# Weight loads on ScalarE's queue, with a planner that knows two queues, in a fused attention and feed-forward kernel

## The chip, the cores and the metric

The kernel runs on one core of one Trainium2 chip. The metric is the device time of one execution in microseconds (us): the median of three runs. The engines are named as the profile names them: PE is TensorE's matmul, PEld its weight load, DVE is VectorE, ACT is ScalarE, POOL is GpSimd, SP is SyncE, whose queue issues DMA transfers. All arithmetic runs in float32; a "split" operand is held as a rounded high part and a low part, so that two or three fast matmuls give a float32 product.

## The reference

The inputs are q, k, v of 4 batches x 8 heads x 576 positions x 64, a memory `M_prev` (64 x 64) and `z_prev` (64) per head, `beta` per head, and the weights `w_in` (512 x 2048) and `w_out` (2048 x 512), which come as float64.

```python
scores = where(causal, -1e9, (q @ k.T) / 8); a = softmax(scores); local = a @ v
q_p = where(q > 0, q, exp(q) - 1) + 1
mem_out = (q_p @ M_prev) / (q_p . z_prev + 1e-6)
attn = g * mem_out + (1 - g) * local            # g = sigmoid(beta), per head
x = attn as 2304 tokens x 512
h = x @ w_in;  g = where(h > 0, h, exp(min(h, 0)) - 1)
out = g @ w_out
```

## The kernel before

The 2304 tokens are cut into nine groups of 256: unit 0 holds the first 64 positions of the four batches, the units 1 to 4 the next 256 positions of one batch each, the units 5 to 8 the last 256. A unit's attention runs over four pairs of heads, and its result is the 512-wide x of the group, split into `xh` and `xl`. The feed-forward of a group runs over 16 chunks of 128 hidden columns: `add_ff` multiplies x by a chunk of `w_in` into the PSUM tile h (L901), applies the elu (ACT L916; DVE L919, L922), splits the result into `gh` (L931) and `gl` (L934) and accumulates its product with the chunk of `w_out` (L965). The groups named by `SPLIT` run their first chunks early and the others later, so that feed-forward work starts while only a few chunks of the weights are ready; the half sums go out to a buffer `part` and come back.

The weights arrive as float64 and are turned into split float32 on the core, piece by piece: 32 pieces (16 chunks of each matrix), 128 x 1024 int32 words each, 512 KB. `add_weights` issues the load into the staging tile `st` (L379; two buffers), then scales the exponent word (rebias, L385, L387 or L389 on ACT, DVE or POOL), isolates the sign (L396 or L398), merges the low word (L403, L406, both on DVE), rounds the high part (L409) and subtracts for the low part (L412). The join L406 is the last reader of the staging buffer, which then takes the load after the next.

In attention, `add_phi` makes q_p (ACT L464, DVE L467 to L496, DVE or POOL L485); unit 0 goes through `add_first` (score matmuls L588, masked reductions L592, exponentials L607, transposes L636, products L651), the others through `add_pair` (scores L787 or L819, reductions L801, exponentials L832, scaling L848, transposes L878, copies L884, products L739). `add_mem` puts the memory's factor beside the probabilities (L545, on DVE or POOL).

Nothing of this is issued in the order of the code. Each operation is handed to a planner (`Plan`), with a priority, the tiles it reads and writes, and one or more engines that could run it, each with an assumed duration. `Plan.order` then keeps one clock per engine and always takes the operation that can begin first, the lower priority number first among equals; of several engines it takes the one that ends first after a bonus in `BIAS`. The order in which it takes them is the order of the instructions on each engine's queue, which is fixed. Where PE would stand idle before the first feed-forward accumulation, the planner puts in warm-up matmuls that compute nothing (L1033). The numbers at the top of the file (`A_OFF`, `V_OFF`, `E_OFF`, `UDUE`, `UBEG`, `W_ADD`, `P_ADD`, `W_LATE`, `SPLIT`) shift priorities: of the units, of the loads of v, of the elu, of the single weight pieces. All DMA transfers stand on SP's queue. An issue waits on its queue until its buffer is free, and what is queued behind it waits too.

## Time and profile before

| what | us |
|---|---|
| time, median of 3 runs (lowest, highest) | 599.02 (598.54, 599.17) |
| profiled execution, its own time | 599.39 |
| its span (first to last instruction) | 597.6 |
| busy in the span: PE | 586.7 (98%) |
| busy: DVE | 442.0 (74%) |
| busy: ACT | 381.1 (64%) |
| busy: POOL | 73.0 (12%) |
| issues of weight loads, first to last start | 3.1 to 158.9 |

Busy times are the union of an engine's instructions; DMA issues, waits and branches are not counted as busy. Matmuls are pipelined, so PE counts as busy while its pipeline is not full. The granted clock of PE is full in all stretches up to the last 20 us. A row of the chain of waits gives the share of a stretch in which the chain that ended last ran on that line; the idle time in brackets of a timeline row is the idle time of that engine before the instruction, with what ended it.

### The profile page before, as it was taken

Reading aid. Unit: us, or ns where it says so; the run is one execution under the profiler, and the core shown is the slowest. Engines: PE = TensorE matmul, PEld = TensorE weight load, DVE = VectorE, ACT = ScalarE, POOL = GpSimd, SP = SyncE. Lnnn points to the kernel's source line nnn. Section 1 sums busy time; section 2 is a strip of 40 time slices with the busy share of each in tenths; the row PEclk is TensorE's granted clock in tenths of the full one; section 3 lists DMA queues with packets and bytes.
Section 4 is the critical chain, followed back from the end, with each engine's and each line's share of the span. In section 5 each row is a group of like instructions: output and inputs, shape, how many; then the busy total and the mean of one; then the engine's idle time right before and its main releaser. Section 6 shows DMA issues by size and latency. Waiting matters only on the chain.

```text
span 597.6 us, 11969 instructions
## 1 busy us (share of the span) xinstructions
PE 586.7 (98%) x4150; PEld 507.0 (85%) x4150; DVE 442.0 (74%) x1394; ACT 381.1 (64%) x1021; POOL 73.0 (12%) x108
## 2 busy tenths in 40 slices
PE   8999999999999999999999999999999999999997
PEld 6766868898898898999888999898889888899996
DVE  6999999999987884477774478687968786444443
ACT  5699889676677872377682377686767776533222
POOL 3333123120011120000120000101111010000000
PEclk9999999999999999999999999999999999999999
DMA  8755756445463332012422022424232323000000
GB/s 264 234 189 183 220 158 209 160 163 185 144 184 113 96 127 72 1 59 90 137 74 59 1 94 74 117 72 154 73 118 74 103 92 103 1 2 28 10 1 36
DMA packets 32813, 63.85 MB, mean 107 GB/s; under 512 B 3568, under 2 KB 17392, under 8 KB 32752
## 3 DMA queue, kind: packets, MB, share of 16 engines
q1 hardware_dynamic: 32752, 63.08, 33.5%
q8 instruction: 33, 0.54, 0.4%
q14 instruction: 28, 0.23, 0.1%
HBM read 56.77 MB, written 6.29 MB: 106 GB/s over the span
## 4 chain that ended last, share of the span: by engine, by line
PE 83%; DVE 12%; ACT 2%; issue 1%; DMA 1%; POOL 0%; DVEq 0%; ACTq 0%; POOLq 0%; SPq 0%
PE acc L965 31%; PE h L901 31%; PE t L739 7%; PE t L878 7%; PE s L787 6%; DVE p L801 2%; DVE st L403 1%; PE acc L1033 1%; DVE wf L406 1%; ACT p L848 1%; DMA p<-in_kqf 1%; DVE gl L934 1%; DVE e L919 1%; DVE p L545 1%; DVE qp L470 1%
## 5 line engine op out<-in xcount | busy, mean ns | idle before, releaser
L901 PE MATMUL h<-xh,w1h 128*128 128x256 f32 x576 | 149.4, 284 | 0.5 <-DVE e L922 0.5
L901 PE MATMUL h<-xl,w1h 128*128 128x256 f32 x576 | 148.1, 281 | 0.0
L901 PEld LDWEIGHTS h<-xh,w1h 128*128 128x128 f32 x576 | 108.4, 188 | 11.9 <-DVE e L922 1.0
L901 PEld LDWEIGHTS h<-xl,w1h 128*128 128x128 f32 x576 | 108.9, 189 | 9.6
L916 ACT ACTIVATE e<-h 128x256 f32<-128x256 f32 x144 | 55.1, 383 | 64.7 <-PE h L901 64.0
L931 ACT CAST gh<-e 128x256 fp32r<-128x256 f32 x143 | 57.8, 404 | 59.2 <-DVE e L922 56.4
L965 PE MATMUL acc<-w2h,gl 128*128 128x512 f32 x288 | 93.5, 403 | 0.0
L965 PE MATMUL acc<-w2h,gh 128*128 128x512 f32 x288 | 92.4, 402 | 0.4 <-ACT gh L931 0.4
L965 PE MATMUL acc<-w2l,gh 128*128 128x512 f32 x288 | 92.8, 402 | 0.0
L901 PEld LDWEIGHTS h<-xh,w1l 128*128 128x128 f32 x576 | 85.0, 189 | 9.2 <-issue 0.5
L901 PE MATMUL h<-xh,w1l 128*128 128x256 f32 x576 | 92.7, 283 | 0.0
L832 ACT ACTIVATE p<-p,mn 128x192 f32<-128x192 f32 (+3 forms) x128 | 78.6, 616 | 18.1 <-DVE mn L801 17.9
L919 DVE TENSOR_SCALAR e<-e 128x256 f32<-128x256 f32 x144 | 43.7, 303 | 51.8 <-ACT e L916 50.4
L934 DVE TENSOR_TENSOR gl<-e,gh 128x256 fp32r<-128x256 f32 x131 | 57.3, 438 | 31.7 <-ACT gh L931 30.9
L884 ACT COPY pth<-t 128x384 f32<-128x384 f32 (+2 forms) x155 | 67.2, 455 | 11.5 <-PE t L878 10.4
L878 PE MATMUL t<-ident,p 128*128 128x128 f32 x448 | 69.3, 274 | 1.2 <-POOL p L852 0.6
L801 DVE CUSTOM_DVE_ANT_0 p<-s,mask 128x192 f32<-128x192 f32 (+3 forms) x128 | 57.9, 476 | 14.8 <-PE s L787 9.7
L878 PEld LDWEIGHTS t<-ident,p 128*128 128x128 f32 x448 | 53.5, 140 | 12.4 <-ACT p L848 2.2
L922 DVE SCALAR_TENSOR_TENSOR e<-h,e 128x256 f32<-128x256 f32 x144 | 60.6, 421 | 2.2
L739 PE MATMUL t<-pth,v 128*64 128x256 f32 (+1 forms) x512 | 54.5, 357 | 1.7 <-ACT pth L884 1.7
L739 PEld LDWEIGHTS t<-pth,v 128*64 128x64 f32 x512 | 34.9, 137 | 20.8 <-ACT pth L884 3.4
L848 ACT ACTIVATE p<-p,rs 128x320 f32<-128x320 f32 (+3 forms) x88 | 47.1, 584 | 6.6 <-DVE rs L556 5.2
(97 smaller groups left out, 818.6 us busy)
## 6 DMA issues: line engine op xcount, KB each, us to landing
kq<-in_kq SPq DMA_DIRECT2D x32, 416.0 KB, 3.1
st<-in_w_in SPq DMA_DIRECT2D x16, 512.0 KB, 3.4
st<-in_w_out SPq DMA_DIRECT2D x16, 512.0 KB, 3.6
qz<-in_qzx SPq DMA_DIRECT2D x32, 224.0 KB, 2.9
v<-in_vx SPq DMA_DIRECT2D x32, 160.0 KB, 2.4
out<-st SPq DMA_DIRECT2D x16, 256.0 KB, 2.1
kq<-in_kqp SPq DMA_DIRECT2D x12, 288.0 KB, 3.3
v<-in_vx SPq DMA_DIRECT2D x16, 192.0 KB, 3.4
```

Source lines behind the costliest of these rows:

```text
L739: nc.tensor.matmul(ps.t[64 * j:64 * j + 64, G * n + lo:G * n + G], vj.t[:, v0 + c], tj.t[:, o:o + G - lo], start=(i == 0), stop=(i == len( ...
L801: nc.vector.tensor_tensor_reduce(out=pts[i].t[:, po + 64 + a:po + 64 + e], in0=ps.t[:, o:o + e - a], in1=m, op0=ALU.add, op1=ALU.min, scal ...
L832: nc.scalar.activation(out=x, in_=x, func=AF.Exp, bias=mn.t[:, 0:1], scale=-1.0, accum_out=rs.t[:, col:col + 1])
L848: eng.activation(out=x, in_=x, func=AF.Copy, scale=c)
L878: nc.tensor.matmul(ps.t[:, 128 * (c - a):128 * (c - a) + 128], pt.t[:, po + 128 * c:po + 128 * c + 128], ident, start=True, stop=True, is_ ...
L884: return lambda: eng(dst(), ps.t[:, 0:n].rearrange("p (c q) -> p c q", q=128))
L901: nc.tensor.matmul(ps.t[:, 0:G], w[:, c, k], x.t[:, k], start=(k == 0 and w is w1h and x is xh), stop=(k == 3 and lo))
L916: nc.scalar.activation(out=at(ee), in_=ps.t[:, 0:G], func=AF.Exp)
L922: nc.vector.scalar_tensor_tensor(at(gg), ps.t[:, 0:G], 0.0, e.t, ALU.max, ALU.add)
L931: return lambda: eng(gh.t, at(gg))
L934: return lambda: eng.tensor_tensor(gl.t, at(gg), gh.t.bitcast(F32), op=ALU.subtract)
L965: nc.tensor.matmul(acc[t].t, a.t[:, 128 * t:128 * t + 128], w[:, c], start=(c == c0 and i == 0), stop=(c == c1 - 1 and i == 2))
```

## The change

The load of a weight piece is issued by `nc.scalar` in place of `nc.sync`, so it stands on ACT's queue. The planner gets a second queue, "Q2", which takes 1587 ns per piece as SP did, and for the issue 330 ns of ACT's time; the transfer follows the issue without delay, and its data counts as landed 2600 ns after its end. In the planner both queues have the full rate. Thirteen of the constants at the top are set anew; `PS_FROM`, `RELU_FF` and `PHI_MIN` are among them, which select nothing at the old or the new value. Line numbers below the table of latencies grow by 3 or 4 (L379 becomes L382, L464 becomes L468).

```diff
--- before.py
+++ after.py
@@ -28,31 +28,31 @@
 SIGN = -0x80000000
 REBIAS = 2.0 ** -112
 MASKED = -8e9
-A_OFF = 11
-PS_FROM = 276
+A_OFF = 12
+PS_FROM = 252
 TURN_S = 400.0
 TURN_V = 370.0
 NATIVE = (1, 1, 1, 1, 0, 0, 0, 0, 0)
 PV_TWO = [0, 0, 0, 1, 1, 1, 1, 1, 1]
 RUN_SPLIT = (((0, 0, 192),), ((1, 0, 320),)), (((0, 0, 448),), ((1, 0, 288),), ((1, 288, 576),))
 CLOCK_OFF = 450.0
-V_OFF = 80
+V_OFF = 65
 SN = 2
 TN = 2
-SPLIT = (4, 7, 11)
-UDUE = (-29, 4, 17, 55, 62, 81, 65, 101, 114)
-UBEG = (-44, -1, 11, 22, -4, 67, 91, 58, 99)
+SPLIT = (4, 8, 11)
+UDUE = (-21, 4, 17, 55, 62, 80, 69, 104, 112)
+UBEG = (-50, 0, 12, 22, -12, 67, 89, 61, 99)
 RB = {'mn': 10, 'rs': 4, 'p': 2, 'pth': 4, 'v': 4, 'ks': 1, 'qh': 1, 'ql': 1, 'kq': 1, 'ev': 3}
-BIAS = {'POOL': -400, 'DVE': -150, 'DV2': -250, 'ACT': -750}
-E_OFF = 162
+BIAS = {'POOL': -400, 'DVE': 50, 'DV2': -250, 'ACT': -750}
+E_OFF = 190
 FIRST_ACT = 4
 W_FIRST = -970
-RELU_FF = -20
+RELU_FF = -22
 RELU_PHI = 0
-PHI_MIN = -1
-W_LATE = (1, 0, -4, -14)
-W_ADD = (0, 6, -1, 0, -1, -2, -8, 3, 1, -3, -3, -1, 5, 11, -8, 0, 4, -5, 1, 8, 16, -16, -5, 2, -10, 1, 2, 7, -10, -18, 1, 1)
-P_ADD = (-19, -2, 17, 2, -1, 0, -1, 1, 0, -1, 0, 0, 0, -1, -1, -2, -10, 18, -15, -1, 0, 0, 1, -17, 0, -10, 7, -7, 10, -2, 8, 9, 5, 10, 0, -1)
+PHI_MIN = 0
+W_LATE = (0, 0, -7, -15)
+W_ADD = (-11, 14, -1, 2, 15, -2, -16, 3, 9, -3, -11, -2, 5, 5, -5, -1, 4, -6, 1, 15, 16, -8, 6, 2, -1, 2, 2, 18, -8, -20, -5, -1)
+P_ADD = (-11, 8, 24, 7, -1, 0, -1, 9, 0, -2, 3, 0, 0, 7, -1, -2, -11, 20, -15, -3, -3, 1, -2, -17, 0, -10, 3, -10, 13, 2, 8, 9, -3, 18, 8, -1)
 W_OFF = 4
 SLACK = 0
 WARM_BEG = 1100.0
@@ -67,7 +67,10 @@
     "DVE": {"PE": 200.0, "ACT": 128.0, "DVE": 127.0, "POOL": 203.0, "SP": 200.0},
     "POOL": {"PE": 190.0, "ACT": 130.0, "DVE": 100.0, "POOL": 97.0, "SP": 200.0},
     "SP": {e: DMA_LAT for e in ("PE", "ACT", "DVE", "POOL", "SP")},
+    "Q2": {e: DMA_LAT for e in ("PE", "ACT", "DVE", "POOL", "SP")},
 }
+for _l in LAT.values():
+    _l["Q2"] = 0.0
 
 
 class Ring:
@@ -376,7 +379,7 @@
             return raw.t.rearrange("p (n t) -> p n t", t=2)
 
         def load():
-            nc.sync.dma_start(out=raw.t, in_=src.bitcast(I32))
+            nc.scalar.dma_start(out=raw.t, in_=src.bitcast(I32))
 
         def rebias(eng):
             def g():
@@ -412,7 +415,8 @@
             return lambda: eng.tensor_tensor(dl, f.t.bitcast(F32), dh.bitcast(F32), op=ALU.subtract)
 
         wh, wl = f"w{which}h{c}", f"w{which}l{c}"
-        add(pl, [("SP", dma(512), load)], w=[raw])
+        add(pl, [("ACT", 330, load)], w=[raw])
+        add(pl, [("Q2", dma(512), lambda: None)], w=[raw])
         add(p, [
             ("POOL", pool1(512), rebias(nc.gpsimd)),
             ("ACT", act(512), rebias(nc.scalar)),
```

The counts on the engines change little. ACT has 32 DMA issues more, SP 32 less. 14 of the small products L545 move from DVE to POOL, five of the weight casts L409 and three of the elu's casts L931 from ACT to DVE, eight casts of the attention's split operands L759 and L767 from DVE to ACT, and PE has 136 warm-up matmuls instead of 134.

The first place is the beginning of ACT's queue. `st` is the staging tile of a weight piece, `wf` the piece under work, `qp` the exponential of q, `p`, `rs` and `mn` the probabilities, their sums and minima of one pair. Before:

```order
L464 ACT_TABLE_LOAD
L464 ACTIVATE qp<-qz 128x256 x2
L607 ACTIVATE p,rs<-p,mn 128x64 x2
L1051 ACTIVATE igate<-igate 128x32
L607 ACTIVATE p,rs<-p,mn 128x64 x2
L385 ACTIVATE wf<-st 128x512
L607 ACTIVATE p,rs<-p,mn 128x64
L385 ACTIVATE wf<-st 128x512
```

and now:

```order
L382 DMA st<-in_w_in 128x1024
L382 DMA st<-in_w_out 128x1024
L388 ACT_TABLE_LOAD
L388 ACTIVATE wf<-st 128x512
L468 ACTIVATE qp<-qz 128x256 x2
L611 ACTIVATE p,rs<-p,mn 128x64
L388 ACTIVATE wf<-st 128x512
L1055 ACTIVATE igate<-igate 128x32
L611 ACTIVATE p,rs<-p,mn 128x64 x6
```

Two weight loads stand ahead of the table load, and the rebias of the first piece ahead of the two exponentials of q.

The second place is the beginning of DVE's queue, where ISA is the masked reduction of the scores `s` or the reading of its accumulator. Before:

```order
L467 TENSOR_SCALAR qp<-qp 128x256
L592 ISA p,mn<-s,mask 128x64
L592 ISA mn 128x1
L470 SCALAR_TENSOR_TENSOR qp<-qz,qp 128x256
L592 ISA p,mn<-s,mask 128x64
L592 ISA mn 128x1
L481 TENSOR_TENSOR qz<-qp,qz 128x256
```

and now:

```order
L399 TENSOR_SCALAR st<-st 128x512
L471 TENSOR_SCALAR qp<-qp 128x256
L596 ISA p,mn<-s,mask 128x64
L596 ISA mn 128x1
L474 SCALAR_TENSOR_TENSOR qp<-qz,qp 128x256
L596 ISA p,mn<-s,mask 128x64
L596 ISA mn 128x1
L485 TENSOR_TENSOR qz<-qp,qz 128x256
```

The sign operation of the first weight piece, which follows ACT's rebias of the same piece, is now the first instruction.

The third place is ACT's queue around its first elu exponential (`e<-h`). `xh` is the rounded part of x, `pth` the transposed probabilities, `gh` the rounded part of the elu. Before:

```order
L530 CAST xh<-t 128x256
L464 ACTIVATE qp<-qz 128x256
L409 CAST w1h<-wf 128x512
L916 ACTIVATE e<-h 128x256
L848 ACTIVATE p<-p,rs 128x192
L848 ACTIVATE p<-p,rs 128x320 x2
L884 COPY pth<-t 128x2x128
L884 COPY pth<-t 128x3x128
L931 CAST gh<-e 128x256
L884 COPY pth<-t 128x2x128
L832 ACTIVATE p,rs<-p,mn 128x192
```

and now:

```order
L534 CAST xh<-t 128x256
L852 ACTIVATE p<-p,rs 128x192
L852 ACTIVATE p<-p,rs 128x320
L852 ACTIVATE p<-p,rs 128x192
L468 ACTIVATE qp<-qz 128x256
L888 COPY pth<-t 128x2x128
L888 COPY pth<-t 128x3x128
L382 DMA st<-in_w_out 128x1024
L920 ACTIVATE e<-h 128x256 x2
L888 COPY pth<-t 128x2x128
L888 COPY pth<-t 128x3x128
L836 ACTIVATE p,rs<-p,mn 128x192
```

A weight load stands ahead of the first elu exponential, two of which are now together, and more of the attention's copies and scalings are ahead of them.

## Rows read from the trace of the kernel before

**Rows 1.** The page, section 1: busy time, share of the span, instructions.

```profile
PE 586.7 (98%) x4150; PEld 507.0 (85%) x4150; DVE 442.0 (74%) x1394; ACT 381.1 (64%) x1021; POOL 73.0 (12%) x108
```

**Rows 2.** Busy time by stretch: its length, busy time per engine, PEclk, DMA share, GB/s.

```profile
34.00:110.00 76.00, 72.44 (x493) 55.23 (x492) 74.67 (x240) 66.52 (x200) 19.59 (x27) 1.00 0.58 188
110.00:190.00 80.00, 80.00 (x540) 69.90 (x539) 71.50 (x205) 55.89 (x146) 11.56 (x14) 1.00 0.51 160
...
2.00:8.00 6.00, 5.68 (x58) 4.03 (x57) 2.40 (x16) 2.34 (x12) 0.53 (x2) 1.00 0.98 335
```

**Rows 3.** Chain of waits from 34, 110, 190 and 310 us on: shares of the stretch.

```profile
by line: DVE p L801 9.5%; PE acc L965 7.4%; DVE wf L406 7.3%; PE h L901 7.2%; DVE st L403 7.0%; ACT p L848 6.8%; issue 4.1%; DVE gl L934 4.0%; DVE e L922 3.8%; DVE p L545 3.6%; DVE e L919 3.5%; ACT pth L884 3.4%; DVE w2l L412 3.1%; DVE xl L
...
by line: PE acc L965 43.8%; PE h L901 41.3%; PE t L739 5.8%; PE t L878 5.0%; PE s L819 2.7%; PE s L787 1.9%
...
by line: PE h L901 35.7%; PE acc L965 35.2%; PE t L878 9.5%; PE s L787 8.5%; PE t L739 7.2%; DVE gl L934 0.7%; issue 0.6%; DVE ks L762 0.6%; ACT p L848 0.6%; DVE qz L485 0.4%; DVE qp L470 0.3%; DVE rn L489 0.3%; DVE e L919 0.2%; DVE rs L553
...
by line: PE acc L965 35.7%; PE h L901 35.6%; PE t L739 10.0%; PE t L878 8.7%; PE s L787 8.2%; DVE p L801 0.4%; DVE e L919 0.4%; DVE ks L762 0.3%; DVE ks L759 0.2%; DVE qp L470 0.2%; DVE e L922 0.1%; DVE gl L934 0.1%; DVE ql L770 0.1%; DVE q
```

**Rows 4.** Line L379, the weight loads: issue min/median/max ns; who waited for them.

```profile
L379 SPq DMA_DIRECT2D st<-in_w_in x16: 327/328/458, 3.1 to 156.2; - x16
...
  POOL wf L389: 1.3, 2
```

**Rows 5.** SP's waits from 0 to 110 us: us in total, times, longest.

```profile
SPq L379 <- DVE wf L406: 16.5, 8, 4.4
```

**Rows 6.** Timeline of SP from 0 to 21 us: start, us, engine, line, operation.

```profile
3.06 0.43 SPq L379 DMA_DIRECT2D st<-in_w_in  x1
...
15.83 0.34 SPq L567 DMA_DIRECT2D p<-in_kqf  x1
```

**Rows 7.** Timeline of ACT, DVE and PE, four instructions before 21 us; idle time in brackets.

```profile
5.97 0.42 ACT L464 ACTIVATE qp<-qz 128x256 f32<-128x256 f32 x1 [1.44 <-DMA qz<-in_qzx]
...
5.89 0.23 DVE L592 CUSTOM_DVE_ANT_0 p<-s,mask 128x64 f32<-128x64 f32 x1 [1.03 <-PE s L588]
...
9.83 0.21 DVE L592 CUSTOM_DVE_ANT_0 p<-h,mask 128x64 f32<-128x64 f32 x1
...
20.43 0.68 PE L588 MATMUL h<-p 64*64 64x64 f32 x16 [0.75 <-DMA p<-in_kqf]
```

**Rows 8.** DVE's waits from 0 to 34 us.

```profile
DVE qp L467 <- ACT qp L464: 4.6, 1, 4.6
...
DVE p L592 <- PE h L588: 0.5, 1, 0.5
DVE p L801 <- PE t L636: 0.4, 1, 0.4
```

**Rows 9.** Instructions by form, DVE and ACT: busy us, mean ns, idle time before.

```profile
L934 DVE TENSOR_TENSOR gl<-e,gh 128x256 fp32r<-128x256 f32 x131 | 57.3, 438 | 31.7 <-ACT gh L931 30.9 <-PE t L878 0.5
...
L403 DVE SCALAR_TENSOR_TENSOR st<-st 128x512 int32<-128x512 int32 x32 | 22.2, 697 | 0.7 <-POOL st L398 0.7
...
L848 ACT ACTIVATE p<-p,rs 128x320 f32<-128x320 f32 x29 | 15.8, 554 | 0.0
...
L545 DVE TENSOR_TENSOR p<-qp,rn 128x128 f32<-128x128 f32 x39 | 12.4, 321 | 8.5 <-PE t L878 8.2
...
L412 DVE TENSOR_TENSOR w1l<-wf,w1h 128x512 fp32r<-128x512 f32 x15 | 11.2, 746 | 0.4 <-ACT w1h L409 0.4
...
L409 ACT CAST w1h<-wf 128x512 fp32r<-128x512 f32 x14 | 8.7, 619 | 2.4 <-DVE wf L406 2.2
...
L409 DVE CAST w1h<-wf 128x512 fp32r<-128x512 f32 x2 | 0.8, 420 | 0.0
```

**Rows 10.** Pieces of the chain on PE: start, us, engine, line, instructions.

```profile
191.26 0.55 PE t L878 x5
...
210.56 2.40 PE h L901 x20
```

## The prediction

> **What bounds the kernel now.** I read the page first. TensorE (PE) is busy for 98% of the span [rows 1], but the page warns that a busy PE is not PE at its peak, so the next views were the busy times by stretch and the chain of waits by stretch [rows 2, 3]. The reader is to see two kernels in one. From 34 to 110 us DVE is busy 74.67 of 76 us and ACT 66.52; in the chain of that stretch the first two PE entries hold 7.4% and 7.2%, and the rest is spread over DVE and ACT lines. From 110 us on the chain is PE: its entries add up to 100% until 190 us, 96% until 310 us and 98% until 593 us. So PE's own work is the floor after 110 us, and the time is decided by how much of PE's work is done when DVE stops holding it back, which is near the 12th of the 144 feed-forward chunks (counted by DVE's L922). Then I read the loads: SP's timeline, what SP's weight loads wait for, and who waits for them [rows 4 to 6]. The weights are late for nobody: their landing holds up only POOL, for 1.3 us in the whole program [rows 4], and POOL is busy for only 12% of the span [rows 1]. What gates them is the staging ring of two buffers: SP stood 16.5 us in 8 waits at L379 for DVE's join L406 in the first 110 us [rows 5]. So a second queue removes no wait that the chain shows. It can act in three ways: at the start, where the DMA engines are full (335 GB/s and 98% busy from 2 to 8 us, [rows 2]); through ACT's time; and through the order that the newly set constants give.
>
> **The start.** Before, SP issues kqf, qz, qz, kqf and beta ahead of the first two weight loads, the first of which goes out at 3.06 us [rows 6]. Now ACT issues both weight loads as its first instructions, beside SP's first two loads. ACT gets qz of the second pair at 5.97 us [rows 7], when kqf, qz and qz (0.77 MB) have landed. If the two queues share byte for byte, as much of the weights goes along: 0.77 MB at 335 GB/s is 2.3 us, so that qz lands near 8.3. In ACT's order the first weight's rebias and both qp now stand ahead of the first exponential, and DVE's first instruction is the weight's sign, which waits for that rebias. w_in (0.52 MB) and the first kqf and qz (0.52 MB) are then all done when 1.05 MB have moved, 1.6 us after the 0.52 MB that were enough for that qz before; DVE, which first worked at 4.56 us [rows 8], starts near 6.2. Its first reduction on the second pair began at 9.83, in work without a break since 5.89 [rows 7]; 20 instructions stood ahead of it, 4.0 us with the one at 4.56, and 11 do now, by the same durations 2.5 us. It can begin near the same 9.8, since the second kqf also lands later, so DVE is 1.5 us of work behind there. Part comes back: before, DVE stood 0.5 and 0.4 us for the fourth pair's scores and for a transpose behind them [rows 8], because that pair's kqf, issued at 15.83 [rows 6], landed only when its matmuls began at 20.43 [rows 7]. A DVE that is 1.5 us late finds it there. So +0.6 us. The ends: -0.3 if SP's queue is served first and a third of the 0.9 comes back all the same; +2.0 if that kqf, with one more v load ahead of it and half a megabyte of the next w_in beside it, slips by 0.7 MB (2.1 us at the same rate).
>
> The Trainium skill, "DMA: Bandwidth & Descriptors", section "Issuing engines are not separate DMA queues", says that loads issued by several engines run on the same 16 DMA engines and interleave, so that all one saves is the issuing sequencer's time. The 335 GB/s of the full stretch and the 1.3 us that anybody waits for weights agree with it. By that rule alone the edit's own worth is nil and only its side effects count; a reading as two separate bandwidths would have left the start term at zero or below.
>
> **ACT's time.** An issue takes SP 0.328 us in the median [rows 4]. The trace has no issue on ACT, so I bound it: 0 if it runs beside ACT's arithmetic, 0.33 if ACT stands. Up to the 12th chunk ACT's order now holds 17 of the 32 issues, 17 x 0.33 = 5.6 us. It loses other work at the same point: five 320-wide probability scalings (5 x 0.47) and two weight casts (2 x 0.54; means of [rows 9] less the 0.08 by which an instruction overlaps the next), and the other kinds add 0.2: 3.2 us less. Net +2.4 us at the upper end, -3.2 at the lower. ACT's idle time from 34 to 110 us is 9.5 us [rows 2], which covers it on the average; what isn't covered is an ACT instruction behind an issue that waits for DVE's join. SP had 16.5 us of such waits, but the planner now places each issue where it expects the buffer to be free. I take +0.3 us; the ends are 0 (cover holds; a lighter ACT gains nothing while DVE is the fuller engine) and +2.4.
>
> **The new order.** The PE work is the same instruction for instruction, but for 136 warm-up matmuls instead of 134, in gaps anyway. At the 12th chunk DVE has eight fewer small products L545 (8 x 0.24 = 1.9; they moved to POOL), two fewer L934 (0.7) and two more casts L409 (0.7), and the other kinds cancel: 1.9 us less [rows 9]. But PE has then done less too: 12 L901 fewer (12 x 0.12) and 5 L878 fewer (5 x 0.11), 2.0 us [rows 10]. What counts is DVE's time up to a chunk plus PE's work after it: -1.9 + 2.0, nothing. At the 22nd chunk DVE has 1.9 us less (L545 -1.9, L934 -0.7, L403 and L412 -1.3, L409 +1.4, the rest +0.6) and PE 16 L901 more and 5 L878 fewer done (1.9 - 0.5 = 1.4): a lead of 3.3 us. It is gone by the 40th chunk. In before's stretch with these chunks, 110 to 190 us, the chain is all PE already [rows 3], so a lead buys little: -0.4 us, between 0 and -1.2. From 190 us on the chain holds 3.9% of 120 us and 1.8% of 283 us outside PE, 4.7 + 5.1 us; a reordered attention may take away or add a quarter of that, 0 +- 2.4.
>
> **The sum.** +0.6 + 0.3 + 0 - 0.4 + 0 = +0.5 us on the profiled execution's 599.39 us: 599.9. The median of the runs is 0.37 lower, 599.02, so on its scale 599.5.
>
> **The rivals.**
> Faster: the order wins. For it: DVE is the full engine until 110 us, POOL with its 12% takes the eight L545, and q loads no longer queue behind weight loads on SP. If the 1.9 us of DVE work show in full, because PE's 12 matmuls fit into gaps it has anyway, the start term is eaten by the stall at 20 us and the mid lead yields its 1.2: -1.9 - 1.2 + 0.3 = -2.8, which is 596.2. Against it: the sum at the 12th chunk is level, and gaps of PE after 110 us are few.
> Slower: ACT becomes the bound between 34 and 110 us. Its mechanism: an issue stands at the head of ACT's queue until DVE's join frees the staging buffer, and behind it wait the casts xh and gh that PE needs and the exponentials. The price is ACT's net 2.4, with the start at 1.5 and the order at -0.4: +3.5, which is 602.5. It decides once ACT's 9.5 us of idle time are spent, that is if each of the 14 or so issues of the stretch costs 0.9 us with its wait (9.5 + 3.2 by 14). For it: ACT is already busy 88% there. Against it: ACT's own waits are mostly for DVE, so an issue that waits for DVE waits in their place.
> Not what it says: the weights land no earlier after the first two, since the two buffers gate them. That is likely, and it is in the forecast, which expects nothing from earlier weights.
>
> **How the numbers follow.** The forecast, no change, has 0.40, the faster rival 0.31, the slower one 0.29. A change of 0.2% (1.2 us) is about what a measurement of this kernel tells from none: 597.8 to 600.2 is "same". The forecast's own range is 597.5 to 601.0; of its 0.40, 0.32 fall within, 0.02 below and 0.06 above. So faster 0.33, same 0.33, slower 0.34 (of each rival a little falls within). The range for 8 in 10 takes in most of both rivals: 595.6 to 602.6; its ends lie 0.6 below the faster rival's time and at the slower one's.
>
> **What would show it.** Start: ACT's second qp after 7.5 us and DVE's first reduction of the second pair after 9.5 us; if that qp still starts near 6, the start term is wrong. ACT: its issues in the timeline with idle time of ACT at most 0.4 us each, and a PE wait list as short as before; if "ACT gh" or "ACT xh" enters the chain of 34 to 110 us with more than 5%, the slower rival holds. Order: DVE's busy time per stretch within 1 us until 110, and a 12th L922 within 1.5 us of the old place; if it comes 2 us earlier with as much PE work done, the faster rival holds. The forecast is wrong altogether if PE waits for a weight.

## The result, and the profile after

| | runs | median, us (lowest, highest) | ratio to the kernel before, 95% interval |
|---|---|---|---|
| before, beside the first measurement | 4 | 598.83 (598.54, 599.17) | |
| changed, first measurement | 3 of 4 | 602.69 (602.33, 603.33) | 1.0067 [1.0053, 1.0081] |
| changed, second time | 6 | 602.41 (601.59, 603.99) | 1.0064 [1.0046, 1.0083] |
| changed, third time, another chip | 4 | 603.30 (602.74, 604.46) | 1.0084 [1.0070, 1.0098] |

The change made the kernel slower by 0.6 to 0.8%, about 4 us; the forecast was no change, 599.5. One execution of the first measurement took 2032.91 us and is left out; the profile had been taken of that one, so the profile after is that of the second time. Its execution took 602.74 us, 3.35 more than the profiled one of before, with a span of 600.9.

What answers to [rows 1 and 2], first the page's busy times, then the three stretches (34 to 110, 110 to 190, 2 to 8 us; columns as there). Line numbers are 3 to 4 higher than before.

```profile
PE 586.0 (98%) x4152; PEld 508.4 (85%) x4152; DVE 444.4 (74%) x1387; ACT 379.5 (63%) x1016; POOL 75.3 (13%) x120
```

```profile
34.00:110.00 76.00, 71.05 (x498) 55.13 (x498) 73.58 (x240) 64.06 (x193) 25.80 (x39) 1.00 0.61 189
110.00:190.00 80.00, 79.76 (x524) 70.12 (x523) 74.96 (x203) 49.50 (x129) 10.53 (x15) 1.00 0.49 153
2.00:8.00 6.00, 4.78 (x35) 3.16 (x33) 1.38 (x8) 2.29 (x4) 0.53 (x2) 1.00 1.00 371
```

From 34 to 110 us PE is less busy than before by 1.4 us, DVE by 1.1, ACT by 2.5. An engine that has become the bound would be busier; here all three wait more. Two narrower stretches show where. Before:

```profile
0.00:34.00 34.00, 30.92 (x330) 24.82 (x331) 27.47 (x123) 21.82 (x76) 11.16 (x21) 1.00 0.76 247
60.00:85.00 25.00, 24.95 (x175) 19.54 (x175) 24.53 (x84) 22.57 (x69) 3.88 (x7) 1.00 0.63 199
```

and after:

```profile
0.00:34.00 34.00, 29.18 (x314) 23.43 (x315) 25.65 (x114) 21.22 (x73) 9.65 (x19) 1.00 0.69 239
60.00:85.00 25.00, 23.06 (x161) 17.70 (x162) 22.90 (x75) 19.44 (x59) 6.74 (x10) 1.00 0.59 176
```

DVE has 1.8 us less done at 34 us, and loses another 1.6 between 60 and 85; PE loses 1.7 and 1.9. The chain of waits from 34 to 110 us [rows 3] has an entry that was not there before, and from 190 us on it is PE alone where 3.9% lay outside PE before:

```profile
by line: DVE wf L409 11.6%; DVE st L406 9.9%; DVE p L805 9.7%; DMA part<-ev 8.4%; issue 6.3%; DVE w2l L415 4.9%; DVE qp L474 4.4%; DVE w1l L415 4.1%; DVE e L926 4.1%; DVE xl L537 3.1%; DVE gl L938 2.9%; DVE st L399 2.9%; DVE rn L493 2.8%; D
...
by line: PE h L905 36.1%; PE acc L969 35.5%; PE t L882 10.0%; PE s L791 9.4%; PE t L743 9.2%
```

"DMA part<-ev" is the store of partial sums. `ev` is a ring of three buffers: ACT and DVE copy the accumulator into one (L1023), SP stores it (L1026), and the next copy into the same buffer waits until that store has landed. DVE's side of it, with the weight load on ACT's queue and SP's issues ahead of it:

```profile
64.82 0.34 ACTq L382 DMA_DIRECT2D st<-in_w_in  x1
...
64.75 0.33 SPq L465 DMA_DIRECT2D qz<-in_qzx  x1
65.17 7.21 SPq L1026 DMA_DIRECT2D part<-ev  x4
...
71.61 0.42 DVE L1023 COPY ev<-acc 128x256 f32<-128x256 f32 x1 [1.92 <-DMA part<-ev]
```

The load went out at 64.82, the first store 0.35 us behind it, and DVE stood 1.9 us before its copy. The start, for [rows 7]:

```profile
7.73 0.42 ACT L468 ACTIVATE qp<-qz 128x256 f32<-128x256 f32 x1 [0.71 <-DMA qz<-in_qzx]
...
5.83 0.43 DVE L399 TENSOR_SCALAR st<-st 128x512 int32<-128x512 int32 x1 [5.83 <-ACT wf L388]
...
10.14 0.15 DVE L596 CUSTOM_DVE_ANT_0 p<-h,mask 128x64 f32<-128x64 f32 x1
...
8.45 0.68 PE L592 MATMUL h<-p 64*64 64x64 f32 x16 [1.68 <-DMA p<-in_kqf]
9.07 3.34 PE L1037 MATMUL acc<-ident 128*128 128x256 bf16 x29
```

The second q exponential begins at 7.73 (before 5.97), DVE's first instruction at 5.83, and its first reduction of the second pair at 10.14 (before 9.83).

To add up such losses I weigh each PE instruction with its pace (119 ns for an h, 231 for an acc, 109 for a transpose, and so on; [rows 10] show two of them) and take, at a time t, the work that PE still has to do in a run less that in the kernel before. I call it PE's lag; it is good to some 0.5 us. All runs that follow are in this table; the last column is the time's median less that of before in the same comparison.

```
lag of PE, us, at             40    60    70    80   100   150   590   time
changed                      1.2   1.5   1.5   3.6   3.2   3.2   2.9   +3.5
changed, third time          1.9   1.6   2.2   4.6   4.2   4.2   3.8   +4.8
all loads on SyncE           5.1   3.9   5.8   6.6   6.0   6.1   6.5   +4.4
first two on ScalarE         1.9   1.5   1.6   2.7   2.2   2.2   1.9   +2.1
before, loads on ScalarE    -0.2   0.3   0.2   0.1   0.1  -0.4   0.2   +1.2
one load on SyncE            1.9   1.5   2.2   2.7   2.1   2.2   1.4   +2.9
first two planned on SyncE   1.2   2.0   6.5   7.0   6.4   6.7   6.3   +8.9
code without constants       1.5   0.3   0.7   1.6   1.0   2.9   7.3   +8.5
constants without code       0.0   0.1   0.8   1.3   0.3   0.6   0.1   +1.0
later start                  0.2   1.0   0.5   2.7   2.1   2.0   1.6   +4.0
before, two loads first      1.7   1.7   2.2   2.3   1.6   1.9   1.9   +2.8
both repairs                 0.6   1.0   0.5   0.6  -0.1  -0.1  -0.5   +1.6
both repairs, again          1.2   1.5   1.5   1.7   1.2   1.0   0.7   +1.5
later start, 30 on SyncE     0.6   0.8   0.2   1.0   0.6   0.5   0.8   +1.1
all on SyncE, old start      2.2   1.5   1.8   2.3   1.9   1.8   0.9   +2.0
```

The loss of the changed kernel is made in two places: by 40 us, and between 70 and 80. Behind 110 us the lag stays. The lag compares single executions: before's took 599.39 us, 0.4 to 1.0 us above its medians in the comparisons (599.00 to 598.36), so the column of times stands higher than the lag by about that, and by what a run's own profiled execution lies off its median.

### The profile page after: what moved, and what is told of

The parts are those of the page before. It is cut to its first block, busy times and chain, and to the rows that moved or that the text cites. A ratio compares the mean times of both kernels' runs of the same rounds, so it can differ in the third digit from the quotient of the medians.

```text
span 2031.1 us, 11967 instructions
## 1 busy us (share of the span) xinstructions
PE 2025.2 (100%) x4152; PEld 1401.0 (69%) x4152; DVE 453.2 (22%) x1387; ACT 393.8 (19%) x1016; POOL 72.4 (4%) x120
## 3 DMA queue, kind: packets, MB, share of 16 engines
HBM read 56.77 MB, written 6.29 MB: 31 GB/s over the span
## 4 chain that ended last, share of the span: by engine, by line
PE 100%; POOL 0%; DVE 0%; issue 0%; POOLq 0%
PE h L905 35%; PE acc L969 35%; PE t L743 9%; PE t L882 9%; PE s L791 6%; PE acc L1037 3%; PE s L823 2%; PE t L655 0%; PE h L592 0%; PE acc L640 0%; PE s L592 0%; PE t L640 0%; DVE st L1001 0%; POOL mask L1043 0%; POOL ident masks.py:199 0%
## 5 line engine op out<-in xcount | busy, mean ns | idle before, releaser
L905 PE MATMUL h<-xh,w1h 128*128 128x256 f32 x576 | 396.1, 688 | 0.0
L905 PE MATMUL h<-xl,w1h 128*128 128x256 f32 x576 | 393.1, 683 | 0.0
L905 PEld LDWEIGHTS h<-xl,w1h 128*128 128x128 f32 x576 | 258.6, 449 | 95.0 <-issue 89.6
L905 PEld LDWEIGHTS h<-xh,w1h 128*128 128x128 f32 x576 | 254.4, 442 | 89.0 <-issue 78.2
L905 PEld LDWEIGHTS h<-xh,w1l 128*128 128x128 f32 x576 | 240.7, 451 | 81.5 <-issue 74.9
L969 PE MATMUL acc<-w2h,gl 128*128 128x512 f32 x288 | 284.4, 1117 | 0.0
L969 PE MATMUL acc<-w2l,gh 128*128 128x512 f32 x288 | 281.0, 1106 | 0.0
L905 PE MATMUL h<-xh,w1l 128*128 128x256 f32 x576 | 280.4, 695 | 0.0
L969 PE MATMUL acc<-w2h,gh 128*128 128x512 f32 x288 | 279.2, 1103 | 0.0
L882 PE MATMUL t<-ident,p 128*128 128x128 f32 x448 | 212.6, 686 | 0.0
L743 PEld LDWEIGHTS t<-pth,v 128*64 128x64 f32 x512 | 62.4, 242 | 122.5 <-issue 113.4
L969 PEld LDWEIGHTS acc<-w2l,gh 128*128 128x128 f32 x288 | 125.0, 457 | 19.9 <-issue 15.5
```

Of the source, the lines that this page charges most:

```text
L743: nc.tensor.matmul(ps.t[64 * j:64 * j + 64, G * n + lo:G * n + G], vj.t[:, v0 + c], tj.t[:, o:o + G - lo], start=(i == 0), stop=(i == len( ...
L882: nc.tensor.matmul(ps.t[:, 128 * (c - a):128 * (c - a) + 128], pt.t[:, po + 128 * c:po + 128 * c + 128], ident, start=True, stop=True, is_ ...
L905: nc.tensor.matmul(ps.t[:, 0:G], w[:, c, k], x.t[:, k], start=(k == 0 and w is w1h and x is xh), stop=(k == 3 and lo))
L969: nc.tensor.matmul(acc[t].t, a.t[:, 128 * t:128 * t + 128], w[:, c], start=(c == c0 and i == 0), stop=(c == c1 - 1 and i == 2))
```

## The experiments

Three theories were tried first. Start: the first weights share the DMA engines with q and k. ACT: the 30 later issues make ACT's casts and exponentials late. Order: the new constants give a worse order.

**The changed kernel again.** No edit.

> The changed kernel once more, for an undisturbed profile and its time in five rounds. Measured first: 603.0 us against 598.8, 4.2 us slower. Three theories for the 4.2 us. Start: the first two weight loads go out on ScalarE at once and share the full DMA engines with the first q and k loads; then VectorE's and TensorE's work in the first 30 us is late by 3 us or more, and the lag stays the same from there on. ACT: the 30 later issues, each standing at the head of ScalarE's queue, make the casts and exponentials late; then the lag grows between 34 and 110 us, with ScalarE's idle time in front of its issues. Order: the new constants give a worse order of the same work; then the lag grows in a stretch where the issues have no wait in front of them, or after 110 us.

602.41. It gave the profile above: both the start and a step inside 34 to 110 us, but no idle time of ACT in front of its issues.

**The same order on SyncE.** Two kernels keep the changed order on every engine and differ only in who issues.

```diff
-            nc.scalar.dma_start(out=raw.t, in_=src.bitcast(I32))
+            if c == 0:
+                held.append((raw, src))    # issued by nc.sync right behind beta
+            else:
+                nc.sync.dma_start(out=raw.t, in_=src.bitcast(I32))
```

and, in the second,

```diff
-            nc.scalar.dma_start(out=raw.t, in_=src.bitcast(I32))
+            (nc.scalar if c == 0 else nc.sync).dma_start(out=raw.t, in_=src.bitcast(I32))
```

> The changed kernel's order on every engine, but all 32 weight loads are issued by SyncE again, the first two right behind the load of beta as in the kernel before. Start: back near 599 (598.5 to 600). ACT: back near 599 as well. Order: it stays near 603 (602 to 604).

> The changed kernel's order; ScalarE issues only the first two weight loads (at its start), SyncE issues the other 30 at the same place of the plan. Start: it stays near 603. ACT: back near 599 to 600. Order: near 603, the same as with all loads on SyncE.

With all on SyncE 603.29 (1.0084 [1.0067, 1.0102]), with two on ScalarE 601.06 (1.0042 [1.0028, 1.0056]). The first lies where the order theory had put it (602 to 604), but it is no clean test of the order: its VectorE begins with the sign of a weight, which now comes behind beta, so that it stood 9.4 us at the start, PE stood 3.6 us for a probability, and its granted clock fell from 1.00 to 0.51 (waits from 0 to 34 us, then two stretches):

```profile
DVE st L402 <- ACT wf L391: 9.4, 1, 9.4
...
PE t L643 <- ACT p L614: 3.6, 1, 3.6
```

```profile
10.00:14.00 4.00, 1.40 (x13) 1.00 (x11) 4.00 (x26) 2.58 (x12) 0.64 (x1) 1.00 0.81 265
14.00:18.00 4.00, 3.02 (x14) 2.21 (x14) 3.86 (x19) 2.68 (x10) 0.00 (x0) 0.51 0.81 232
```

The second is a test: the 30 later issues on ScalarE cost 1.35 us (602.41 less 601.06), and 2.1 stay with the start and the order. On SyncE's queue these loads also stand at another place among SyncE's stores. In its profile VectorE doesn't wait for the store.

**The old order on ScalarE's queue.**

```diff
-            nc.sync.dma_start(out=raw.t, in_=src.bitcast(I32))
+            nc.scalar.dma_start(out=raw.t, in_=src.bitcast(I32))
```

> The kernel before with its own constants and its own order; the one edit is that ScalarE issues the 32 weight loads at the places where the plan had SyncE issue them. Start: 602 to 603, if the first two are then issued at once as in the changed kernel. ACT: 601 to 604, since the plan of before does not know of the issues' time and places them without regard to ScalarE. Order: within 1 us of 599.

600.08 (1.0024 [1.0014, 1.0033]): under the 601 of ACT and the 602 of start, and just outside order's 1 us. Start's condition, both loads at once, isn't met: the first weight load here goes out at once, but w_out only at 6.35 us, and no lag is left at 40. The lag at the end is 0.2 where the median of 11 runs is 1.2 higher; most of that lies in which executions were profiled, this one 0.4 us below its median and before's 0.5 above. Its order is that of before instruction for instruction, so one place can be compared directly: a weight load and three stores, the first of them issued 0.37 us behind the load. The profile lists the issues from 62.4 to 66.7 us (KB each, median us from issue to landing), first before:

```profile
st<-in_w_in SPq DMA_DIRECT2D x1, 512.0 KB, 3.8
part<-ev SPq DMA_DIRECT2D x3, 128.0 KB, 3.7
qz<-in_qzx SPq DMA_DIRECT2D x1, 224.0 KB, 3.3
```

then with the load on ScalarE's queue:

```profile
st<-in_w_in ACTq DMA_DIRECT2D x1, 512.0 KB, 5.6
part<-ev SPq DMA_DIRECT2D x3, 128.0 KB, 5.1
qz<-in_qzx SPq DMA_DIRECT2D x1, 224.0 KB, 4.8
```

On one queue the load had landed in 3.8 us and the stores behind it; on two all land later, the load still first, the stores after 5.1. But this pair doesn't show that the second queue made them later. In the kernel before with only the first two loads on ScalarE (run below) this load stands on SyncE's queue, ahead of the same three stores, and they took nearly as long (issues from 64.6 to 69 us):

```profile
st<-in_w_in SPq DMA_DIRECT2D x1, 512.0 KB, 5.0
part<-ev SPq DMA_DIRECT2D x3, 128.0 KB, 4.9
```

In the run at hand VectorE's next copy to that buffer began at 69.14 us, by when they had landed: no wait. In the changed kernel the landings are later still, and the copy would have begun 4.5 us after the first store's issue where it began 6.0 after it before and here:

```profile
st<-in_w_in ACTq DMA_DIRECT2D x1, 512.0 KB, 6.6
part<-ev SPq DMA_DIRECT2D x3, 128.0 KB, 6.1
...
qz<-in_qzx SPq DMA_DIRECT2D x1, 224.0 KB, 6.5
```

**One load moved.** i counts the pieces; 10 is the one of 64.82 us.

```diff
-            nc.scalar.dma_start(out=raw.t, in_=src.bitcast(I32))
+            (nc.sync if i == 10 else nc.scalar).dma_start(out=raw.t, in_=src.bitcast(I32))
```

> The changed kernel, but a single weight load, the eleventh (the sixth of w_in), is issued by SyncE at its place in the plan, which is behind the first of four stores of partial sums; in the changed kernel ScalarE issued it at 64.8 us, 0.35 us ahead of the first store, and the four stores landed 6.4 us later and kept VectorE's next copy to that buffer waiting for 1.9 us. If that meeting is what the other 30 loads cost on ScalarE's queue: the first store lands in 2 to 3.5 us, VectorE's wait of 1.9 us is gone, and the time is 601.1 (600.7 to 601.5), as with 30 loads on SyncE. If it is the issue time on ScalarE, spread over all loads: 602.3, as the changed kernel.

601.28, as expected of the meeting. The first store now lands in 2.8 us, DVE's list of waits has no store in it, and the lag at 80 us is 2.7 in place of 3.6:

```profile
st<-in_w_in SPq DMA_DIRECT2D x1, 512.0 KB, 5.3
...
part<-ev SPq DMA_DIRECT2D x1, 128.0 KB, 2.8
```

The edit changes two things, the queue and with it the place. In the plan this load stands behind the first store, and on SyncE's queue it goes out there (store at 65.85 us, load at 66.33). On ScalarE's queue nothing kept it behind: the store waited on SyncE for ScalarE's copy to `ev`, which ran from 64.77 to 65.12, and the load went out at 64.82. In all seven profiles of this order in which SyncE issues the load, the first store lands 2.5 to 3.4 us after its issue, and the two stores behind the load, on the same queue, after 4.4 to 5.5. So the first store is late because the load went out ahead of it; that a second queue adds to this isn't shown. A load on ScalarE's queue behind the first store was not run.

On that chip before ran at 598.36, so the ratio, 1.0047 [1.0033, 1.0061], overlaps the changed kernel's; the profile decides, and the run with both repairs below.

**The planner asked again.** Three kernels in which the plan is made anew: the first two loads planned on SyncE, the code without the constants, the constants without the code.

```diff
-        add(pl, [("ACT", 330, load)], w=[raw])
+        add(pl, [("SP", dma(512), load) if c == 0 else ("ACT", 330, load)], w=[raw])
...
-A_OFF = 12      (code without constants: this and the other twelve back;
+A_OFF = 11       constants without code: the change's diff above its class Ring only, without Q2)
```

> The changed kernel, but the planner gives the first two weight loads to SyncE, so that it plans the start for them there; the other 30 stay with ScalarE, the constants stay as changed. If the start costs 1.8 us because VectorE's first instruction waits for a weight that shares the DMA engines with q and k: VectorE first works near 4.6 us, is busy 27 us of the first 34 again (25.6 in the changed kernel, 27.5 in the kernel before), and the time falls by 1 to 2 us, to 600.4 to 601.4. If the loss is the constants alone: 602 or more. The plan behind the start shifts as well, so that the stores may meet a load elsewhere.

> The second queue in code and planner, but with the constants of the kernel before. If the start and the meeting of loads with stores make the loss: VectorE's first instruction waits for a weight again and 1 us or more is lost by 34 us, 600.5 to 603. If the constants make it: within 1 us of 599.

> The kernel before with SyncE's one queue and a planner that knows only that queue, but with the new constants. If the start and the meeting make the loss: 599 to 600.5, VectorE busy 27 us of the first 34. If the constants make it: 602 or more.

607.30 (1.0147 [1.0128, 1.0166]), 606.88 (1.0137 [1.0119, 1.0156]) and 599.37 (1.0012 [0.9999, 1.0024]). The constants on the old queue are harmless or nearly so, which speaks against the constants, though the order that they give there is not the changed kernel's. The other two came out far above the times expected of the start; 607.30 would be the constants by its stated condition (602 or more), but the profiles show something else: each new plan loses in a place of its own, the first 4.5 us of lag from 60 to 70, the second 5.9 from 100 to 250, where the changed kernel loses next to nothing. Such a kernel doesn't isolate a term; the next ones leave the plan alone and move instructions in the finished list.

**A later start.** In the changed plan w_out's load (piece 1) goes behind the second q exponential (ex0.1), the first weight's rebias to the place of the second's, its sign behind VectorE's first reduction, and the second's rebias and sign behind the third q exponential. The run with both repairs adds the line of the one load moved.

```diff
+        for x, after in (("load1", "ex0.1"), ("rebias0", "rebias1"), ("sign0", "red0.0"), ("rebias1", "ex0.2"), ("sign1", "rebias1")):
+            fns.remove(tag[x])
+            fns.insert(fns.index(tag[after]) + 1, tag[x])
```

> The changed kernel with the order of its first microseconds alone altered: ScalarE still issues w_in first, but w_out, the first weight's rebias on ScalarE and its sign on VectorE stand behind the first two q exponentials and VectorE's first reduction; all else is in the changed order. If the start costs what TensorE's lag at 40 us shows (1.2 us in the changed kernel's profile, 1.9 with the 30 loads on SyncE) because q lands behind the weights: the second q exponential starts near 6 us, the lag at 40 us is 0.5 us or less, and the time falls by 0.7 to 1.4 us against the changed kernel, 601.0 to 601.7 where that one has 602.4. If what is lost early is made up later anyway: no change.

> Both repairs in one: the first microseconds as in the run with the later start of the weights, and the eleventh weight load on SyncE behind the first store. If start and store are the whole loss, and the rest of the new order costs nothing: 599 to 600, at most 1.2 us above the kernel before. If the new order costs something of its own: 601 or more.

> The kernel before in its own order and with its own constants; only the first two weight loads are issued by ScalarE as its first instructions. The rebias and sign of the weights stay where they were, behind the first exponentials. If sharing the DMA engines is the cost: the second q exponential starts at 7.5 us or later, as in the changed kernel (7.73), TensorE lags 1 us at 40 us, and the time is 600 or a little more. If it is the order of VectorE's and ScalarE's first instructions that costs: q lands late as well, but the time stays within 0.5 us of 599.

> The changed kernel once more on the chip of these runs, as the base for the two repairs: 602.4, a ratio of 1.006 to 1.007 to the kernel before; in the profile the first store lands 5 us or more after its issue and VectorE waits 1.5 us or more for it, if the meeting with the weight load is not an accident of one execution.

On one chip: changed 603.30 (602.4 was expected; VectorE stood 2.1 us for the store again), later start 602.52 (1.0063 [1.0050, 1.0075]), later start and the one load moved 600.11 (1.0031 [1.0020, 1.0042]). The later start alone gains 0.8 on the changed kernel beside it, at the lower end of the 0.7 to 1.4 expected, with the second q exponential at 6.29 us and a lag of 0.2 at 40 us; the store still keeps VectorE waiting, 1.8 us. Both together take away 3.2 of the 4.8 us (expected 599 to 600, missed by 0.1), and in the profile all of it, though the profiled execution, 599.25, is the fastest of its seven:

```profile
0.00:34.00 34.00, 29.37 (x320) 23.56 (x321) 25.83 (x118) 21.53 (x75) 10.17 (x20) 1.00 0.72 247
60.00:85.00 25.00, 25.00 (x180) 20.09 (x177) 24.75 (x82) 21.61 (x64) 7.03 (x11) 1.00 0.64 198
```

PE is busy through all of 60 to 85 us again, and the span is 597.5, before 597.6. The third kernel goes the other way: the kernel before, with only the first two loads moved to ScalarE's beginning.

```diff
-            nc.sync.dma_start(out=raw.t, in_=src.bitcast(I32))
+            (nc.scalar if c == 0 else nc.sync).dma_start(out=raw.t, in_=src.bitcast(I32))
...
-        for fn in plan.order(SLACK):
+        for fn in early + [f for f in fns if f not in early]:    # early: these two loads
```

It costs 2.8 us, 601.31 (1.0043 [1.0031, 1.0056]), more than the "600 or a little more" expected, with a lag of 1.7 at 40 us. Its second q exponential begins as late as the changed kernel's, although its VectorE has no weight in front:

```profile
7.84 0.42 ACT L466 ACTIVATE qp<-qz 128x256 f32<-128x256 f32 x1 [0.55 <-DMA qz<-in_qzx]
```

So it is the sharing of the DMA engines that costs at the start, and with only one of the two loads at once (the old order on ScalarE's queue) there was no lag at 40 us.

**What stays.** The last three kernels put the rest of 1.5 us to the second queue or to the order: the repaired start with 30 loads, and with all loads, on SyncE, and both repairs again.

```diff
-            nc.scalar.dma_start(out=raw.t, in_=src.bitcast(I32))
+            (nc.scalar if c == 0 else nc.sync).dma_start(out=raw.t, in_=src.bitcast(I32))
...
+            nc.sync.dma_start(out=raw.t, in_=src.bitcast(I32))    # all: the first two moved behind beta,
+                                         # the first rebias and sign behind the fourth exponential
```

> The changed order with the repaired start (ScalarE issues the first two weight loads, w_out behind the q exponentials); the other 30 loads are on SyncE. If the rest of 1.5 us is the second queue: 598.5 to 599.3, level with the kernel before. If it is the order: 600 or more.

> The changed order behind a start as in the kernel before: all 32 loads on SyncE, the first two behind beta, the first weights' rebias and sign behind the first exponentials. With all loads on SyncE but the changed start this order took 603.3. If start and second queue are the whole loss and the order's lead of some 0.6 us is real: 598 to 599, level with the kernel before or slightly faster. If the order costs something: 600 or more.

> Both repairs, with 29 loads on ScalarE, once more on the chip of these runs: 600.1, a ratio of 1.002 to 1.004 to the kernel before, as the first time.

600.09 (1.0018 [1.0008, 1.0027]), 600.99 (1.0028 [1.0017, 1.0040]) and 600.48 (1.0025 [1.0016, 1.0034]). None is level with before, so the second queue isn't the rest, or not most of it: 29 loads on ScalarE and two differ by 0.4 us, and their intervals overlap. By the conditions set, 600.09 and 600.99 both put the rest on the order. The profile of both repairs differed this time, with a lag of 1.2 us at 40 against 0.6: the start varies from one execution to the next. In the kernel with all loads on SyncE the lag of 2.2 us stems from the first 40 us too. Which part of the order makes the 1 to 2 us, and whether it makes them all, stays open; no version here beats the kernel before.

## Why the prediction was wrong

**The term of ACT's time, +0.3, is the step that failed: it put what an issue does to other transfers at nothing.** It asked what 32 issues cost ACT, and named only ACT's neighbours as those who could be late. For ACT it was right: an issue takes 0.334 us, and its wait for the buffer 17 ns in the median,

```profile
L382 ACTq EVENT_SEMAPHORE  x17: 17/17/1177, 19.9 to 164.9; - x17
L382 ACTq DMA_DIRECT2D st<-in_w_in x16: 334/335/408, 0.7 to 161.6; - x16
```

of the 17 after the first two that go out before 110 us, 12 lie beside ACT's arithmetic, and ACT was busy for 2.5 us less from 34 to 110 us where 3.2 less were forecast up to the 12th chunk. The prediction read that a second queue saves nothing but issue time, and made of it that "only its side effects count", but looked for these in the first 10 us alone. The store of partial sums, which ends a wait of DVE, is such a side effect: between 70 and 80 us the lag grew by 2.1 us (2.4 in the other profile), of which 0.4 came back by 100. From 70 to 100 us it grew by 1.6 to 2.0 us in the three profiles with this meeting, where VectorE stood 1.8 to 2.1 us for the store, and by -0.6 to 0.6 in the seven of the same order in which SyncE issued the load behind the store. Moving the one load lowered the time over before by 0.6 us in one pair of runs and by 2.4 in the other, which ran on one chip. So the mechanism is shown, with about 1.7 us of lag on the average of these profiles. ScalarE's queue is what let the load go out ahead of the store. The answer was in reach: three buffers for `ev` in the code, four stores in a row, and a copy of VectorE behind them.

**The start, +0.6, had its mechanism right and its size wrong.** q of the second pair was put at 8.3 us and came at 7.73, DVE's start at 6.2 and came at 5.83, and the first reduction was to come after 9.5 (10.14). DVE, to be 1.5 us behind and then 0.6, was 1.8 behind at 34 us. What failed is the 0.9 that was to come back at the fourth pair: DVE's two waits there are gone, as forecast, but after its first instruction it waits 2.3 us in all by 34 us, mostly for ACT, where it had waited 1.9 before. PE's lag at 40 us is 1.2 in one profile and 1.9 in the other, at the upper end, +2.0. The second number holds a cost that the sum had not at all. In that execution PE stood 2.12 us for the second kqf, its granted clock then went down to 0.50, the lower of its two levels, and came back near 11.7 us:

```profile
8.39 1.12 PE L592 MATMUL h<-p 64*64 64x64 f32 x16 [2.12 <-DMA p<-in_kqf]
9.44 4.44 PE L1037 MATMUL acc<-ident 128*128 128x256 bf16 x29
```

```profile
9.00:10.00 1.00, 1.00 (x13) 0.75 (x10) 0.86 (x4) 0.85 (x6) 0.65 (x1) 0.50 1.04 399
10.00:11.00 1.00, 1.00 (x7) 0.70 (x5) 1.00 (x9) 0.72 (x4) 0.00 (x0) 0.50 1.04 379
...
12.00:13.00 1.00, 1.00 (x12) 0.90 (x10) 1.00 (x9) 0.44 (x2) 0.00 (x0) 1.00 1.01 357
```

In the first profile it stood 1.68 us and the clock stayed at 1.00; 29 warm-up matmuls took 3.34 us there and 4.44 here. The length of the wait alone doesn't tell the two apart: with only the first two loads on ScalarE PE stood 1.74 us, and the clock fell to 0.50 as well:

```profile
8.51 0.68 PE L592 MATMUL h<-p 64*64 64x64 f32 x16 [1.74 <-DMA p<-in_kqf]
9.13 5.00 PE L1037 MATMUL acc<-ident 128*128 128x256 bf16 x29
```

Of the five profiles in which ScalarE issues both loads first, four have the lower clock and a lag of 1.7 to 1.9 at 40 us; the fifth has 1.2.

**The order: 0 at the 12th chunk and -0.4 by the 22nd.** Borne out behind the first 40 us. The 12th L922 (now L926) ended at 101.4 us, 0.9 later than before, inside the 1.5 allowed. With start and store repaired the lag goes from 0.6 at 40 us to -0.1 at 150 and -0.5 at the end (from 1.2 to 1.0 and 0.7 the second time). In its first 40 us the order isn't free: with all loads on SyncE and the old start it has a lag of 2.2 there and takes 2.0 us more than before, a cost that the sum didn't have. The late stretch, 0, holds too: from 150 us on the lag stays within 0.6 us of 3.15, and from 190 us the chain is all PE.

**The sum.** Predicted +0.6 + 0.3 + 0 - 0.4 = +0.5; in the profile 1.2 by 40 us, 2.1 between 70 and 80, and -0.4 for all the rest, 2.9 of lag, and 0.4 more behind PE's last matmul, 3.3 of the span.

**The rivals.** The slower one named 602.5 and was within 0.2 us of the first measurement, by luck, for a wrong reason: its issues had to cost ACT 0.9 us each with their wait, but up to 110 us only two waited for the buffer noticeably (1.2 us at 19.9, 0.3 at 92.5); ACT's busy time fell, and "ACT gh" and "ACT xh" have less than 2.8% of the chain each, since its entries stand by size. Its price for the start, 1.5, was the better one. The faster rival's sign, a 12th chunk 2 us earlier, didn't come. Of the signs, DVE's busy time within 1 us per stretch told it at once (60 to 85 us: 1.6 less). The sign that PE waits for a weight was a poor one. It does:

```profile
PE t L882 <- ACT p L852: 1.9, 2, 1.3
PE acc L969 <- DVE w2h L412: 0.8, 1, 0.8
...
PE h L905 <- ACT w1h L412: 0.6, 2, 0.4
PE acc L969 <- DVE ev L1023: 0.5, 1, 0.5
```

but with both repairs it still waits 2.2 us for weights by 110, without a lag: there other waits of PE have gone in exchange.

## What to carry to other kernels

When a transfer moves to another queue, go through every DMA whose landing releases an engine, stores and small rings first, and ask which of them will now share the engines with it, and which it may now overtake: the order that one queue kept between a store and a load is gone on two. Issue time was the smallest part of the price here. Count a delay at the start in full unless a wait behind it is long enough to absorb it, and look whether it opens a gap of TensorE. To test one term of a planned kernel, move instructions in the finished list: the plans made anew for two tests took 5 us more over before than the changed kernel, lost in other places.

## What the runs showed of the hardware

Two queues gave up the planned order of issue, and not the order of landing: in the changed kernel the load overtook the store that stood ahead of it in the plan, went out 0.35 us before it on the other queue, and the store landed 6.4 us after its issue, 0.2 us after the load. Behind a 512 KB load a 128 KB store was late on one queue too: in before's order of instructions (apart from the first two loads in one of the runs) the load and the three stores took 3.8 and 3.7 us in one run and 5.0 and 4.9 in another, both on one queue, and 5.6 and 5.1 on two. The short store didn't overtake the long load in any of them. Part of the long landings is a stretch in which little moved (in the changed kernel below 64 GB/s from 65.9 to 67.1 us); why, no run here shows.

The Trainium skill, "DMA: Bandwidth & Descriptors", section "Issuing engines are not separate DMA queues", says that such loads interleave on the same 16 DMA engines, and the trace agrees (98 to 100% busy and 335 to 371 GB/s from 2 to 8 us on one or two queues). Its section "Queues, rings and completion order" says that each DMA engine takes turns between queues, a packet at a time. The changed kernel's trace agrees from 67 to 68.5 us, with the weight load on ScalarE's queue (q10) and, all but a few packets, q on SyncE's (q1):

```profile
q10 hardware_dynamic: 58, 0.24, 45.3%
q1 hardware_dynamic: 70, 0.12, 28.8%
```

The columns are packets, MB and busy share. In this trace a packet is one row, 4096 bytes of the load and 1792 of q, so nearly equal numbers of packets gave the load twice the bytes.

An issue on ScalarE mostly runs beside its arithmetic: of 17 issues of 0.334 us before 110 us, 12 left no gap of 0.2 us in ACT's work.

The start of one kernel isn't one number: two profiles of the same program, both repairs, had lags of 0.6 and 1.2 us at 40 us.
